# Attention and two expert layers in one kernel: raw weights staged in accumulators, values loaded ahead of keys, a smaller filler quota

## The chip, the cores and the metric

The kernel runs as one program on one core of a Trainium2 chip. The metric is device time in microseconds, the median of several runs. Engines are named as in the profile: PE (TensorE) with its weight loads PEld, DVE (VectorE), ACT (ScalarE), POOL (GpSimd) and SP (SyncE), which here only issues transfers.

## The reference

Everything is float32. Three layers follow one another over 2304 tokens of width 512:

```
attention: 4 batches, 8 heads of 64; 512 local and 32 global tokens per batch
  local queries see keys within 32 positions and the 32 global keys
  global queries see everything; softmax(q k^T / 8) v
experts 1: P = exp(x w_gate - max), eight times scaled by row sums and column sums
  out = sum over 8 experts e of P[:, e] * (relu(x w1[e]) w2[e])      w1 512x1024, w2 1024x512
layer 2: elu(x w_in) w_out                                            512x2048, 2048x512, 64-bit weights
```

## The kernel before

**Precision.** Each operand of a large product is split into a high and a low part (`split`, L121: ACT casts the high part, POOL subtracts to get the low part), and three products stand for one (`three`, L129: lines 131, 133 and 135 of the profile).

**Attention.** The 16 head pairs (4 batches by 4 pairs) run in a loop over p; a *pair* below is one turn of it, p = 0 to 16, and a *slot* is one of its eight steps i = 0 to 7. At the start of a turn PE gets the scores of pair p (`scores`, tile s) and the value products of pair p-1 (`pv`, tile o); in odd turns also the global queries' value products and scores (tiles o and sg). In slots 0, 1, 3 and 4 DVE takes the maxima and ACT the exponentials (`maxi`, tile e); in slots 4 and 6 PE transposes the exponentials (`transp`, tile ptp) and ACT copies them (tile pt). In slot 6 of odd turns `expo_g` runs the global exponentials on DVE and ACT (tile eg). In slot 7 of even turns outputs are transposed into the next layer's input x (`x_t`). Batches 0 and 1 of x stay in SBUF, the later ones are stored to scratch by `x_out` (tensors xdh and xdl).

**Filler.** Each slot ends with `fill_for(FILL)`: a generator (`filler`) that issues matmuls of the first expert layer as soon as a batch of x is there, until their planned durations reach the quota. It does unit 0 (half of expert 0) and then unit 1 for batches 0 and 1, in halves of 256 tokens: `mm1` (four groups of 12 matmuls into a bank of the pool psm, which has two; ACT's Relu writes hh, DVE writes hl), then `mm2_part` into a bank that is freed by the groups before, added into the accumulators `accs`. Before x exists (the first four turns), `busy` keeps PE at work with matmuls on zeros. What is left of the filler runs behind the attention. `logits` computes the gate for a batch (tiles lgp, lt, lgt), and when the last batch is through, the row and column sums of the gate (`sinkhorn`, matmul pcs on tile cs) are issued between other matmuls by a planned clock, one step about every 3.9 us; at the first completed output of unit 2 what is left of them is issued at once (`mix2`).

**Weights of units 0 and 1.** `load_unit` is a generator of ten steps: step i loads raw tile i (128x512, 256 KB) into a pool of three buffers and splits raw tile i-2 into wA. For unit 0 a step is taken in slots 1 and 5 of turns 0 to 4. For unit 1 the steps are taken inside `unit_plain`: two where the second half of unit 0 of batch 1 begins, four between its mm2 matmuls, four between the first mm1 matmuls of unit 1.

**Transfers.** All loads and stores are issued on SP in the order of the program: keys and queries of a pair (`load`, tile kq, 592 KB, three buffers), values (`load_vw`, tile vw, 910 KB, two buffers), values for the global queries (`load_vc`, tile vc, one buffer, odd turns), queries of the global tokens (qg). SP waits for a free buffer where none is there, and what is behind waits with it. Eight semaphores serve the transfers in turn. The masks, `first_sums` (tiles sfh and sfl) and the loads for unit 2 are on the same queue.

After the filler every further unit runs in `mix1` and `mix2`, with 512 columns per matmul, and then layer 2; nothing of that is touched.

Of the kernel before, what the change touches and what calls it, by code (L numbers as in the profile page):

```python
# [11 lines left out]
F32 = mybir.dt.float32  # L12
# [22 lines left out]
LEAST, MOST = (float(np.uint32(x).view(np.float32)) for x in (0x38000000, 0x47EFFFFF))  # L35
VN = HD + 1
LOC = B * SL
FILL = 750.0
LAG = 3900.0
AHEAD = (3, 5, 7, 9)  # L40
BACK = (15, 17, 19, 21)
# [19 lines left out]
def tile_net(ctx: ExitStack, tc, kq, vw, vc, qg, wg, w1, w2, wi, wo, consts, out):  # L61
    nc = tc.nc
# [41 lines left out]
    wA = {"1" + p: wall[p][:, :2048].rearrange("p (k f) -> p k f", k=4) for p in "hl"}  # L104
# [16 lines left out]
    def split(hi, lo, src, hi_eng="act", lo_eng="pool"):  # L121
        if hi_eng == "act":
            nc.scalar.copy(hi, src)  # L123
        else:
            nc.gpsimd.tensor_scalar(hi, src, 1.0, 1.0, op0=ALU.mult, op1=ALU.mult)
        e = nc.gpsimd if lo_eng == "pool" else nc.vector
        e.tensor_tensor(out=lo, in0=src, in1=hi.bitcast(F32), op=ALU.subtract)  # L127
# [39 lines left out]
    att = ExitStack()  # L167
# [13 lines left out]
    def load(p):  # L181
        a = kq_t[p] = apl.tile([128, NKS + SL], F32, tag="kq", name="kq")
        if p > 0:
            nc.sync.dma_start(a, kq[p])
            return
        for c in (slice(NKS, NKS + 128), slice(0, 192), None, slice(NKS + 128, None), slice(192, NKS)):
            if c is None:
                nc.sync.dma_start(masks, consts[:, 256:].rearrange("p (a f) -> p a f", a=4))
            else:
                nc.sync.dma_start(a[:, c], kq[0][:, c])  # L190
# [6 lines left out]
    def load_vw(p):  # L197
        v = ap2.tile([128, 2, NS - 2, VN], F32, tag="vw", name="vw")
        nc.sync.dma_start(v, vw[p])
        vw_t[p] = v  # L200

    def load_vc(g):
        c = ap1.tile([112, 4, 5, VN], F32, tag="vc", name="vc")
        nc.sync.dma_start(c, vc[g // 2, g % 2])
        vc_t[g] = c
# [27 lines left out]
    def transp(p, r):  # L233
        s = st[p, r]
        ptp = psr.tile([128, 512], F32, tag="r", name="ptp")
        for i in range(4):
            nc.tensor.transpose(ptp[:, i * 128:(i + 1) * 128], s["e"][:, i], ident)
        s["pt"] = ap3.tile([128, 512], F32, tag="pt", name="pt")
        nc.scalar.copy(s["pt"], ptp)

    def pv(p):
# [143 lines left out]
    def unit_plain(u, b, swap=None):  # L385

        for c0 in (0, 256):
            leave, come = (swap is not None and u == v and c0 == 256 * (1 - v) for v in (0, 1))
            hh, hl = (hs[p][:, :, c0:c0 + 256] for p in "hl")
            if leave:  # L390
                next(swap)
                next(swap)
            n = 0
            for r in mm1(wA, lambda p, k: xcols(p, k, b)[:, c0:c0 + 256], 256, hh, hl):
                yield r
                n += 1
                if come and n % 12 == 0:
                    next(swap, None)
            n = 0
            for o in (0, 128):  # L400
                i = b * 4 + (c0 + o) // 128
                ps = psm.tile([128, 512], F32, tag="m", name="m2")
                for r in mm2_part(wA, ps, hh, hl, o, range(4)):
                    yield r
                    n += 1
                    if leave and n % 6 == 0:
                        next(swap)
                if u == 0:
                    nc.vector.tensor_copy(accs[i], ps)
                else:  # L410
                    nc.vector.tensor_tensor(out=accs[i], in0=ps, in1=accs[i], op=ALU.add)
                yield "q"

    rawp = att.enter_context(tc.tile_pool(name="rawp", bufs=3, side="left"))

    def load_unit(u):

        raw = []
        for i in range(10):
            if i < 8:  # L420
                raw.append(rawp.tile([128, 512], F32, tag="raw", name="raw"))
                nc.sync.dma_start(raw[i], (w1, w2)[i // 4][u][:, i % 4])
            if i > 1:
                n, k = "12"[(i - 2) // 4], (i - 2) % 4
                split(wA[n + "h"][:, k], wA[n + "l"][:, k], raw[i - 2])
            yield

    def first_sums(k, c):
# [43 lines left out]
    with tc.manual_schedule():  # L472
        load(0)
        nc.sync.dma_start(ident, consts[:, 0:128])
        load_vw(0)
        load(1)
        load_qg(0)
        nc.sync.dma_start(ones, consts[:, 128:256])
        nc.sync.dma_start(wgf, wg)
        fill = filler()  # L480
        owed = [0.0]
        done = [False]

        def busy(n):

            for _ in range(n):
                nc.tensor.matmul(idle, zeros[:, :128], zeros, start=True, stop=True)

        lgen = {}

        def logits_part(b):

            if b not in lgen:
                lgen[b] = logits(b)
            for _ in takewhile(lambda r: r != "lag", lgen[b]):
                pass

        def fill_for(ns):
            owed[0] = min(owed[0] + ns, 2.0 * ns)
            while owed[0] > 0 and not done[0]:  # L500
                r = next(fill, "end")
                if r == "end":
                    done[0] = True
                elif r == "wait":
                    owed[0] = 0.0
                elif r == "lag":

                    owed[0] = -0.5 * ns
                elif r != "q":
                    owed[0] -= r  # L510

        zeros = hs["l"][:, 3, :512]
        nc.vector.memset(zeros.bitcast(F32), 0.0)
        idle = psm.tile([128, 512], F32, tag="m", name="idle")
        busy(START)
        unit0_weights = load_unit(0)
        ahead = deque(f for k in range(2) for c in range(4) for f in first_sums(k, c))
        for p in range(np_ + 1):
            live, odd, g = p < np_, p % 2 == 1, p // 2
            if live:  # L520
                scores(p)
            if p > 0:
                pv(p - 1)
                o0, o1 = (st[p - 1, r]["o"] for r in range(2))
            if odd:
                if g > 0:
                    global_pv(g - 1, o0[:, 384:384 + VN])
                scores_g(g, o0[:, 288:352])
                load_vc(g)
            if p + 2 < np_:  # L530
                load(p + 2)
            if p + 1 < np_:
                load_vw(p + 1)
            if p % 4 == 2 and p + 2 < np_:
                load_qg(p // 4 + 1)
            for i in range(8):
                if live and i in (0, 1, 3, 4):
                    if i == 4:
                        transp(p, 0)
                    for j in range(2):  # L540
                        maxi(p, i // 3, (i % 3) % 2 * 2 + j)
                if i == 2:
                    if p > 0:
                        norm(p - 1, 0)
                        norm(p - 1, 1)
                    if p == 0:
                        split(wgs[:, :, :E], wgs[:, :, E:], wgf)
                if i == 5 and odd and g > 0:
                    norm_g(g - 1)
                if i == 6:  # L550
                    if live:
                        transp(p, 1)
                    if odd:
                        expo_g()
                    elif p > 0:
                        copies = global_t(g - 1, o1[:, 384:512])
                if i == 7 and not odd and p > 0:
                    copies()
                    x_t(g - 1)
                    if g % 2 == 0:  # L560
                        b = g // 2 - 1
                        st["xready", b] = True
                        if b > 1:
                            x_out(b)
                if i in (1, 5) and p < 5:
                    next(unit0_weights, None)
                if p < H // 2:
                    busy(WARM)
                fill_for(FILL)
                if st.get(("xready", 1)):  # L570
                    pop(ahead)
                if p == 13 and i in (0, 4):
                    logits_part(2)
        og = psr.tile([128, 512], F32, tag="r", name="og")
        global_pv(B * 2 - 1, og[:, :VN])
        norm_g(B * 2 - 1)
        pop(ahead, len(ahead))
        x_tg()
        x_out(B)
        for b in (B - 1, B):  # L580
            for _ in range(2):
                logits_part(b)
                for _ in range(14):
                    next(fill, None)
# [765 lines left out]
```

## Time and profile before

| | us |
|---|---|
| median of 3 runs | 1956.5 (1956.34 to 1960.3) |
| profiled execution | 1957.93 |
| its span, first to last instruction | 1956.2 |
| PE busy | 1901.3 (97%) |
| DVE busy | 1430.7 (73%) |
| ACT busy | 768.8 (39%) |
| POOL busy | 670.5 (34%) |
| raw tiles, issue to landing | 2.8 to 10.4, median 7.2 |

PE is busy nearly all the time over the whole span, but not evenly: the page's row of forty slices begins with 7897989 and goes on with nines. The clock that PE was granted is below full in the first slice and in single short stretches. A busy share of PE therefore says less than the idle time in front of single PE instructions, with the name of what ended it, and the clock of the stretch behind.

### The profile page before, as it was taken

What the parts mean: (1) busy time and instruction counts of PE and PEld (TensorE: products, weight loads), DVE (VectorE), ACT (ScalarE), POOL (GpSimd) and SP (SyncE); (2) the same over time, 40 slices, a digit from 0 to 9 for tenths busy, and PEclk for the clock granted to TensorE, in tenths of its full rate; (3) what the DMA queues carried; (4) which work ended last, traced back from release to release, by engine and by line L of the source; (5) the groups of instructions that cost most, each with busy time, mean ns of one, the idle gap of its engine ahead of it and who ended that gap; (6) DMA issues with size and microseconds to landing.
All of it is one profiled execution on the core that took longest, in us unless ns stands there. A gap on an engine that the chain in (4) does not pass through costs nothing. (4 is left out here: it accounts for less than half of the span.)

```text
span 1956.2 us, 32431 instructions
## 1 busy us (share of the span) xinstructions
PE 1901.3 (97%) x12315; PEld 1638.1 (84%) x12315; DVE 1430.7 (73%) x2707; ACT 768.8 (39%) x1599; POOL 670.5 (34%) x581
## 2 busy tenths in 40 slices
PE   7897989999999999999999999999999999999999
PEld 5776768888888888899999999999999977789998
DVE  3454476676776767687878787888888677778887
ACT  4444333333322323233333333333333244545654
POOL 1035222333223333344435353555455112223322
PEclk9899999999999999999999999999999999999999
DMA  6556521332223322623343434333333495554432
GB/s 238 177 176 216 196 76 44 97 104 77 100 80 108 103 76 76 234 87 111 116 122 113 123 109 133 98 108 99 101 103 103 126 293 166 168 213 139 121 118 71
DMA packets 200716, 250.30 MB, mean 128 GB/s; under 512 B 16752, under 2 KB 150128, under 8 KB 200560
## 3 DMA queue, kind: packets, MB, share of 16 engines
q1 hardware_dynamic: 200560, 248.23, 39.6%
q8 instruction: 97, 1.59, 0.3%
q14 instruction: 59, 0.48, 0.1%
HBM read 189.32 MB, written 58.85 MB: 127 GB/s over the span
## 5 line engine op out<-in xcount | busy, mean ns | idle before, releaser
L131 PE MATMUL m<-w2h,hh 128*128 128x512 f32 x1360 | 534.6, 393 | 6.9 <-DVE hl L140 4.7
L135 PE MATMUL m<-w2h,hl 128*128 128x512 f32 x1360 | 535.0, 393 | 2.5 <-POOL hl L1003 2.5
L133 PE MATMUL m<-w2l,hh 128*128 128x512 f32 x1360 | 534.2, 393 | 0.0
L972 ACT ACTIVATE hh<-t 128x288 fp32r<-128x288 f32 (+1 forms) x368 | 184.9, 502 | 437.0 <-DVE t L966 432.6
L135 PEld LDWEIGHTS m<-w2h,hl 128*128 128x128 f32 x1360 | 256.6, 189 | 59.6 <-POOL hl L1003 5.8
L131 PEld LDWEIGHTS m<-w2h,hh 128*128 128x128 f32 x1360 | 257.1, 189 | 57.5 <-DVE hl L140 5.3
L133 PEld LDWEIGHTS m<-w2l,hh 128*128 128x128 f32 x1360 | 257.0, 189 | 50.8
L974 DVE SCALAR_TENSOR_TENSOR hl<-t,hh 128x288 fp32r<-128x288 f32 (+1 forms) x368 | 283.2, 770 | 4.0 <-ACT hh L972 0.2
L1074 DVE SCALAR_TENSOR_TENSOR acc<-m,pr,acc 128x512 f32<-128x512 f32 x247 | 183.2, 746 | 116.2 <-PE m L135 116.2
L127 POOL TENSOR_TENSOR w2l<-w2r,w2h 128x512 fp32r<-128x512 f32 x120 | 162.7, 1380 | 299.9 <-ACT w2h L123 284.9
L966 DVE TENSOR_TENSOR t<-q,u 128x288 f32<-128x288 f32 (+1 forms) x348 | 182.9, 526 | 62.2 <-PE q L1033 52.9
L1003 POOL TENSOR_TENSOR hl<-eg,hh 128x288 fp32r<-128x288 f32 (+2 forms) x112 | 103.7, 934 | 290.2 <-ACT hh L1002 189.8
L690 ACT CAST wh<-wt 128x512 fp32r<-128x512 f32 x120 | 68.9, 619 | 239.0 <-POOL wt L686 239.0
L686 POOL TENSOR_TENSOR wt<-w1r,wt 128x512 f32<-128x512 f32 x60 | 89.5, 1492 | 203.0 <-DVE hl L974 107.5
L686 POOL TENSOR_TENSOR wt<-w1r 128x512 f32<-128x512 f32 x60 | 79.9, 1335 | 174.7 <-DVE hl L974 124.6
L1014 DVE TENSOR_TENSOR u<-q,s 128x288 f32<-128x288 f32 (+1 forms) x116 | 61.2, 528 | 86.0 <-PE q L1033 61.7
L694 DVE TENSOR_TENSOR wl<-wt,wh 128x512 fp32r<-128x512 f32 x120 | 106.9, 901 | 14.6 <-ACT wh L690 12.9
L1222 DVE TENSOR_TENSOR acc<-m,acc 128x512 f32<-128x512 f32 x105 | 72.1, 688 | 32.8 <-PE m L135 32.5
L760 POOL TENSOR_TENSOR cp<-r,cp 128x512 f32<-128x512 f32 x32 | 42.7, 1335 | 144.0 <-DVE cp L750 73.3
L1012 ACT COPY s<-q 128x288 f32<-128x288 f32 (+1 forms) x116 | 52.0, 448 | 77.6 <-PE q L1033 77.6
L694 DVE TENSOR_TENSOR wl<-w1r,wh 128x512 fp32r<-128x512 f32 x90 | 81.3, 903 | 0.0
L984 ACT ACTIVATE er<-t 128x288 f32<-128x288 f32 (+1 forms) x96 | 48.5, 505 | 81.3 <-DVE t L966 81.2
(238 smaller groups left out, 4160.8 us busy)
## 6 DMA issues: line engine op xcount, KB each, us to landing
w1r<-in_w_dram SPq DMA_DIRECT2D x60, 512.0 KB, 4.9
w2r<-in_w_dram SPq DMA_DIRECT2D x60, 512.0 KB, 3.7
vw<-in_vw_dram SPq DMA_DIRECT2D x16, 910.0 KB, 6.7
wh<-wqh SPq DMA_DIRECT2D x98, 128.0 KB, 2.7
wl<-wql SPq DMA_DIRECT2D x98, 128.0 KB, 2.7
kq<-in_kq_dram SPq DMA_DIRECT2D x15, 592.0 KB, 7.1
r<-in_wo_dram SPq DMA_DIRECT2D x16, 512.0 KB, 3.9
r<-in_wi_dram SPq DMA_DIRECT2D x16, 512.0 KB, 3.6
```

The source lines that it names most:

```text
L127: e.tensor_tensor(out=lo, in0=src, in1=hi.bitcast(F32), op=ALU.subtract)
L131: nc.tensor.matmul(ps, ah, bh, start=first, stop=False)
L133: nc.tensor.matmul(ps, ah, bl, start=False, stop=False)
L135: nc.tensor.matmul(ps, al, bh, start=False, stop=last)
L686: eng.tensor_tensor(out=t, in0=get(a), in1=get(b), op=op)
L694: eng.tensor_tensor(out=wop[n + "l"], in0=src, in1=wop[n + "h"].bitcast(F32), op=ALU.subtract)
L966: nc.vector.tensor_tensor(out=t, in0=ps, in1=rest, op=ALU.add)
L972: nc.scalar.activation(hh, t, AF.Relu)
L974: late.append(lambda: nc.vector.scalar_tensor_tensor(out=hl, in0=t, scalar=0.0, in1=hh.bitcast(F32), op0=ALU.max, op1=ALU.subtract))
L1003: nc.gpsimd.tensor_tensor(out=hl, in0=g[:, a:b], in1=hh.bitcast(F32), op=ALU.subtract)
L1074: nc.vector.scalar_tensor_tensor(out=accs[i], in0=ps, scalar=scale, in1=accs[i], op0=ALU.mult, op1=ALU.add)
L1222: nc.vector.tensor_tensor(out=acc, in0=ps, in1=acc, op=ALU.add)
```

## The change

The quota of a slot falls from 750 to 650. Raw tiles of unit 0 are loaded into the accumulators accs[0] to accs[7], which are not used until the first output of the filler; for unit 1 the pool gets five buffers instead of three, five tiles are loaded in slots 0 to 4 of turn 6, and the last three when the first three splits free a buffer. `load_unit` now has eight steps, each a split. The first split of unit 0 stands in turn 1, slot 1, as before. The pt tile moves to a pool of two buffers. Keys of pair 1 are loaded ahead of the values of pair 0 at the start; in the loop the order becomes values, keys, global values. The split of the gate's weights (wgs) moves from turn 0 to turn 2.

```diff
-FILL = 750.0
+FILL = 650.0
...
-        s["pt"] = ap3.tile([128, 512], F32, tag="pt", name="pt")
+        s["pt"] = ap2.tile([128, 512], F32, tag="pt", name="pt")
...
-            if leave:
-                next(swap)
-                next(swap)
...
-    rawp = att.enter_context(tc.tile_pool(name="rawp", bufs=3, side="left"))
+    rawp = att.enter_context(tc.tile_pool(name="rawp", bufs=5, side="left"))
+    raw = {}
+
+    def load_raw(u, i):
+        raw[u, i] = accs[i] if u == 0 else rawp.tile([128, 512], F32, tag="raw", name="raw")
+        nc.sync.dma_start(raw[u, i], (w1, w2)[i // 4][u][:, i % 4])
 
     def load_unit(u):
 
-        raw = []
-        for i in range(10):
-            if i < 8:
-                raw.append(rawp.tile([128, 512], F32, tag="raw", name="raw"))
-                nc.sync.dma_start(raw[i], (w1, w2)[i // 4][u][:, i % 4])
-            if i > 1:
-                n, k = "12"[(i - 2) // 4], (i - 2) % 4
-                split(wA[n + "h"][:, k], wA[n + "l"][:, k], raw[i - 2])
+        for i in range(8):
+            n, k = "12"[i // 4], i % 4
+            split(wA[n + "h"][:, k], wA[n + "l"][:, k], raw[u, i])
+            if u == 1 and i < 3:
+                load_raw(1, i + 5)
             yield
...
+        load(1)
         load_vw(0)
-        load(1)
...
-                load_vc(g)
+            if p + 1 < np_:
+                load_vw(p + 1)
             if p + 2 < np_:
                 load(p + 2)
-            if p + 1 < np_:
-                load_vw(p + 1)
+            if odd:
+                load_vc(g)
...
-                    if p == 0:
+                    if p == 2:
                         split(wgs[:, :, :E], wgs[:, :, E:], wgf)
...
-                if i in (1, 5) and p < 5:
+                if i in (1, 5) and p < 4:
+                    load_raw(0, 2 * p + i // 4)
+                if i in (1, 5) and 0 < p < 5:
                     next(unit0_weights, None)
+                if p == 6 and i < 5:
+                    load_raw(1, i)
```

Three places in the order of the instructions. The first is SP's queue around the stores of x (xdh, xdl), in turns 12 to 14; raw is a raw tile of unit 1, sfh and sfl are partial sums. Before:

```order
L422 DMA raw<-in_w_dram 128x512 x3
L354 DMA xdh<-hh 512x1x512
L354 DMA xdl<-hl 512x1x512
L204 DMA vc<-in_vc_dram 112x1300
L184 DMA kq<-in_kq_dram 128x1184
L199 DMA vw<-in_vw_dram 128x1820
L422 DMA raw<-in_w_dram 128x512
L446 DMA sfh<-hh 512x1x128
L446 DMA sfl<-hl 512x1x128
L422 DMA raw<-in_w_dram 128x512
```

And after the change:

```order
L354 DMA xdh<-hh 512x1x512
L354 DMA xdl<-hl 512x1x512
L199 DMA vw<-in_vw_dram 128x1820
L184 DMA kq<-in_kq_dram 128x1184
L204 DMA vc<-in_vc_dram 112x1300
L416 DMA raw<-in_w_dram 128x512
L445 DMA sfh<-hh 512x1x128
L445 DMA sfl<-hl 512x1x128
L416 DMA raw<-in_w_dram 128x512 x2
```

Two raw tiles stood behind the stores before, the seventh and eighth of unit 1; three do now, the sixth to the eighth, and values go ahead of keys and global values.

The second is ACT's queue in turn 7, from the exponentials of the second head on (e); m is a bank of the filler, hh the Relu of a group, eg the global exponentials. Before:

```order
L231 ACTIVATE e<-e,m 128x128 x2
L139 ACTIVATE hh<-m_1432 128x256
L239 COPY pt<-ptp 128x512
L295 ACTIVATE eg<-sg,mg 128x480
L295 ACTIVATE eg<-o,mg 128x64
L139 ACTIVATE hh<-m_1462 128x256
L139 ACTIVATE hh<-m_1498 128x256
L231 ACTIVATE e<-e,m 128x128 x6
```

And after the change:

```order
L231 ACTIVATE e<-e,m 128x128 x2
L139 ACTIVATE hh<-m_1420 128x256
L239 COPY pt<-ptp 128x512
L295 ACTIVATE eg<-sg,mg 128x480
L295 ACTIVATE eg<-o,mg 128x64
L139 ACTIVATE hh<-m_1449 128x256
L231 ACTIVATE e<-e,m 128x128 x4
L139 ACTIVATE hh<-m_1485 128x256
L231 ACTIVATE e<-e,m 128x128 x2
L139 ACTIVATE hh<-m_1584 128x256
```

Before, the last two groups of a half stood directly behind the global exponentials; now one group does, and the last two stand in the next turn, between its exponentials.

The third is PE's queue at the end of the column sums, in the first mix2 of unit 2; q is a product of mix1, m an output bank, pcs the column sums. Before:

```order
L135 MATMUL m_3875<-w2h,hl 128x512
L1031 MATMUL q_3816<-xs4h,wh 128x512
L1032 MATMUL q_3816<-xs4l,wh 128x512
L1033 MATMUL q_3816<-xs4h,wl 128x512
L1031 MATMUL q_3816<-xs4h,wh 128x512
L1032 MATMUL q_3816<-xs4l,wh 128x512
L1033 MATMUL q_3816<-xs4h,wl 128x512
L924 MATMUL pcs<-cs,ones 128x8 x2
L131 MATMUL m_3850<-w2h,hh 128x512
```

And after the change:

```order
L1037 MATMUL q_3852<-x22h,wl 128x512
L131 MATMUL m_3864<-w2h,hh 128x512
L133 MATMUL m_3864<-w2l,hh 128x512
L135 MATMUL m_3864<-w2h,hl 128x512
L131 MATMUL m_3864<-w2h,hh 128x512
L133 MATMUL m_3864<-w2l,hh 128x512
L135 MATMUL m_3864<-w2h,hl 128x512
L928 MATMUL pcs<-cs,ones 128x8
L131 MATMUL m_3876<-w2h,hh 128x512
```

The last two column sums stood together behind the product q before; now the last one stands alone, between matmuls of mix2, and the one before it 18 matmuls earlier.

## Rows read from the trace of the kernel before

**Rows 1.** Busy time by stage: stretch, length, PE, PEld, DVE, ACT, POOL busy, clock, DMA.

```profile
0.00:62.60 62.60, 43.91 (x775) 30.95 (x775) 21.38 (x123) 28.50 (x70) 11.52 (x15) 0.86 0.64 222
62.60:218.50 155.90, 139.21 (x2566) 118.47 (x2565) 76.71 (x361) 73.94 (x186) 47.78 (x78) 0.98 0.53 175
244.00:285.00 41.00, 32.89 (x138) 25.66 (x137) 32.54 (x87) 12.32 (x21) 9.70 (x7) 0.92 0.24 83
285.00:1956.20 1671.20, 1662.79 (x8716) 1445.30 (x8714) 1289.56 (x2109) 647.61 (x1308) 597.64 (x478) 1.00 0.38 119
```

**Rows 2.** PE's waits, 62.6 to 285: waiting for what, total us, times, longest.

```profile
PE pcs L924 <- DVE cs L919: 8.1, 6, 2.5
PE lgt L377 <- DVE hl L140: 6.5, 2, 6.2
PE m L131 <- DVE hl L140: 5.5, 5, 2.2
...
PE ptp L237 <- ACT e L231: 0.6, 1, 0.6
```

**Rows 3.** PE's waits, 0 to 62.6.

```profile
PE o L251 <- issue: 8.3, 2, 4.2
PE ptp L237 <- ACT e L231: 5.5, 9, 2.4
```

**Rows 4.** Timeline, turn 13 to 14: start, length, engine, line, what, [idle before <- releaser].

```profile
160.84 1.16 PE L216 MATMUL s<-kq 64*32 64x128 f32 x64
...
162.56 0.53 SPq L354 DMA_DIRECT2D xdh<-hh  x1
...
168.25 0.93 SPq L422 DMA_DIRECT2D raw<-in_w_dram  x1
...
178.62 0.62 ACT L123 CAST w2h<-raw 128x512 fp32r<-128x512 f32 x1 [5.58 <-DMA raw<-in_w_dram]
...
180.04 0.61 PE L377 MATMUL lgt<-ident,lt 16*128 16x16 f32 x4 [6.22 <-DVE hl L140]
...
185.71 1.16 PE L216 MATMUL s<-kq 64*32 64x128 f32 x64
```

**Rows 5.** Busy time and clock of three short stretches.

```profile
178.49:185.32 6.83, 5.28 (x19) 4.58 (x20) 3.10 (x12) 4.88 (x11) 4.46 (x7) 0.50 0.07 22
277.47:284.30 6.83, 4.34 (x12) 3.48 (x12) 3.74 (x14) 3.46 (x6) 0.00 (x0) 0.50 0.00 0
...
40.00:60.00 20.00, 13.58 (x291) 10.07 (x290) 8.93 (x55) 10.76 (x27) 5.44 (x5) 0.80 0.61 212
```

**Rows 6.** Timeline, turn 0: the gate's weights and the transposes behind.

```profile
12.30 0.22 ACT L123 CAST wgs<-wgf 128x32 fp32r<-128x32 f32 x1 [2.70 <-DMA wgf<-in_wg_dram]
...
12.88 0.62 PE L237 MATMUL ptp<-ident,e 128*128 128x128 f32 x2 [2.42 <-ACT e L231]
```

**Rows 7.** Timeline, end of turn 7: ACT and PE.

```profile
99.19 0.66 ACT L295 ACTIVATE eg<-sg,mg 128x480 f32<-128x480 f32 x1 [2.02 <-DVE mg L293]
...
99.95 0.66 ACT L139 ACTIVATE hh<-m 128x256 fp32r<-128x256 f32 x2
...
100.84 0.49 PE L131 MATMUL m<-w2h,hh 128*128 128x512 f32 x1 [2.20 <-DVE hl L140]
```

**Rows 8.** Timeline, PE: first and last two of six column sums that waited.

```profile
255.74 0.39 PE L924 MATMUL pcs<-cs,ones 128*128 128x8 f32 x2 [1.31 <-DVE cs L919]
...
277.17 0.39 PE L924 MATMUL pcs<-cs,ones 128*128 128x8 f32 x2 [2.15 <-DVE cs L919]
280.05 0.59 PE L924 MATMUL pcs<-cs,ones 128*128 128x8 f32 x2 [2.49 <-DVE cs L919]
```

**Rows 9.** Timeline, PE, turn 6: the two groups of transposes.

```profile
79.25 0.60 PE L237 MATMUL ptp<-ident,e 128*128 128x128 f32 x4
...
81.31 1.05 PE L237 MATMUL ptp<-ident,e 128*128 128x128 f32 x4
```

**Rows 10.** Timeline, PE: the second wait without a releaser.

```profile
54.01 0.88 PE L251 MATMUL o<-vw,pt 128*32 128x65 f32 x23 [4.22 <-issue]
```

**Rows 11.** DMA queues, 49 to 55 us: packets, MB, share of 16 engines.

```profile
q8 instruction: 1, 0.02, 0.9%
```

## Prediction

> **What bounds the kernel now.** I read the busy times by stage first [rows 1]. From 285 us to the end PE is busy 1662.79 of 1671.2 us: nothing in the change reaches there, so that stage only shifts. What can move is the first 285 us: 43.91 of 62.6 us busy with a clock of 0.86 while no filler exists, 139.21 of 155.9 with filler, 32.89 of 41.0 around the column sums of the gate. PE is the engine that is filled, so each idle microsecond of PE in front of 285, and each stretch in which its clock is halved, is time of the kernel. The second view is the list of PE's waits in these stages [rows 2 and 3]: 8.1 us for the column sums (pcs), 6.5 for lgt of which one wait is 6.2, 5.5 for m, and in front of that 8.3 us in which PE waited for nothing that the profile shows, and 5.5 us for exponentials. Third, the timeline around the longest ones, to see who was really late.
>
> The 6.2 us wait at 180.04 is put down to DVE, but ACT shows the cause [rows 4]: it stood 5.58 us in front of CAST w2h until a raw tile landed, at 178.6. That tile was asked for at 168.25, behind the stores of x, which began at 162.56. ACT works in order, so the Relu that frees the filler's bank, and with it DVE and PE, stood behind that cast. Right behind the wait the clock is 0.50 for 6.83 us [rows 5].
>
> The sum is made against the profiled execution, 1957.9 us (1956.2 span and 1.7 around it), which is 1.4 above the median of 1956.5.
>
> **The change part by part.**
>
> *Gate split.* In pair 0 ACT waited 2.70 us for the gate's weights, and PE 2.42 us for the exponentials behind them [rows 6]. In pair 2 these weights are long there; the cast (0.22 us) then stands between exponentials of a stage that waits anyway. What is late next are keys and values of pair 1; the keys now go ahead, and the cast of raw tile 0 may have to wait for its tile, but PE's global scores lie over that. -2.2; bounds -2.7 and 0.
>
> *Raw tiles of unit 0 in the accumulators, five buffers for unit 1.* The eight casts of unit 0 stay in the same slots (both generators reach the first split in pair 1, slot 1); only the third-buffer wait of SP goes. For unit 1 five tiles come in pair 6, and three come after the splits that free a buffer. The order shows where: tile 5 is still issued behind the stores, vw, kq and vc, and its cast stands in pair 14, behind that pair's first four exponentials. Before, the late tile landed 178.6 - 160.84 = 17.8 us after the start of pair 13 [rows 4]; the same bytes stand in front of tile 5, so I take 17.8 again. Pair 13 lasted 185.71 - 160.84 = 24.9 us; without the wait (6.2), the half clock behind it (half of 6.83, 3.4) and eight slots that are 0.1 shorter, 14.5. The cast stands some 3 to 4 us into pair 14 (the pair's score and value products, then 17 filler matmuls), so at 17.5 to 18.5: the tile is just there. Tiles 6 and 7 are wanted 3 us later still. I keep 0.5 us of the wait: -(6.2 + 3.4 - 0.5) = -9.1; bounds -9.6, and -4 if ACT still stands some 5 us.
>
> *Less filler per slot: where a half unit ends.* In pair 7 and pair 11 the fourth mm1 group ended in slot 6 or 7 of an odd pair, where ACT has the global exponentials first: hh of the last two groups came behind them at 99.95, and PE waited 2.2 us for a bank (100.84) [rows 7]. With 0.4 before each, this makes 5.2 of the 5.5 us of m's row [rows 2]. In the new order the halves end in pairs 6, 8, 10, 12 and 14, which have no global exponentials; behind those of pair 7 ACT has only one Relu. -4.5, since other places can pinch; bounds -5.2 and 0.
>
> *Less filler per slot: what moves.* From slot 7 of pair 4 to slot 7 of pair 16 there are 97 slots, 9.7 us of filler by the planner's count, and the order has 165 filler matmuls behind the transposes of xg where it had 106. On PE that is the same work in another place, 0. It matters at two ends. Behind the gate's logits there is more filler for the column sums to hide in: before, the four that stood alone and waited cost 8.1 - 2.15 - 2.49 = 3.5, 0.9 each, and the last two were issued as a pair because the schedule ran out, 2.15 and 2.49 [rows 2 and 8]. Now all eight stand alone, three of them in the filler. I leave four at 0.9: 8.1 falls to 3.5, -4.6, and take half of the 3.4 us that the half clock from 277.47 on cost [rows 5]: -6.3 in all; bounds -11.5 (all of both) and 0.
>
> The other end is the cover of the exponentials. In pair 6 the second four transposes took 1.05 us where the first took 0.60 [rows 9], so PE stands there already. Six slots before them are shorter by 0.1 each: up to 0.6 us in each of 11 pairs, 6.6; I take +3.5, bounds 0 and +6.6.
>
> *Values ahead of keys, global values last.* Each of these tiles is used a pair or two later (kq and vw in the next pair but one, vc likewise), and PE's only wait for them was the first keys, so the direct price is 0. pt with two buffers costs nothing: the value products that free one stand in front of the transposes that fill it. What does change is when transfers run. PE's two longest waits of the first stage, 4.2 us each, have no releaser, and in the one before 54.01 the core's DMA engines moved an instruction packet [rows 3, 10, 11] while keys loaded early for an even pair were under way. These keys now come later. -1; bounds -8 (both waits gone) and +4 (one more like them).
>
> The Trainium skill, Runtime: NRT & Kernel Launch, section Instruction fetch mechanics, holds that crossing an instruction block costs one DMA that is mostly hidden. By it this term would be 0 and the sum 1 us higher; the trace has 4.22 us there that nothing else explains.
>
> *Sum.* -2.2 - 9.1 - 4.5 - 6.3 + 3.5 - 1.0 = -19.6; 1957.9 - 19.6 = 1938.3, and I say 1938.
>
> **The rivals.**
>
> *The raw tile is late again.* For it: tile 5 still stands behind two stores of 1 MB, and its cast now has exponentials of the same pair right behind it. Against it: its place is a pair later. If its wait and the half clock stay whole but for 0.5 us: 1938.3 + 8.6 = 1947.
>
> [...]
>
> *The chain binds, not PE.* With less filler each pair lasts as long as DVE, ACT and the transposes need; the cover costs its full 6.6, and the column sums, which are a DVE chain, wait as before. For it: the 0.45 us in pair 6 and DVE busy in 32.54 of the 41 us in question [rows 1 and 9]. Against it: only 0.6 us of waits for exponentials in 156 us [rows 2]. 1938.3 + 3.1 + 6.3 = 1948.
>
> *The instruction waits go too.* With nothing early under way in the even pairs, both 4.2 us waits vanish: 1938.3 - 7 = 1931.
>
> *Nothing is won.* The filler's places are dealt anew, and waits of the same size appear elsewhere; the moved matmuls are neutral: 1956 to 1959.
>
> *Slower: the clock falls in the attention stage.* One mechanism: PE's gaps between the shorter slots grow until the clock is halved again and again. It has a price in the trace: with no filler the clock was 0.80 from 40 to 60 us, with filler it is 0.98 over 155.9 us [rows 1 and 5]. At 0.80, 0.18 of the roughly 147 us that are left of this stage, 26 us: 1938.3 + 26 = 1964. It decides from a mean clock of about 0.84 on, where it eats the whole gain (0.14 x 147 = 21). Against it: a slot still holds 0.65 us of filler, and the stage's waits for exponentials are short.
>
> **How the numbers follow.** The forecast has 0.57, the late tile 0.15, the chain 0.12, the instruction waits 0.06, nothing won 0.05, the clock 0.05. The forecast's own range is 1932 to 1944 (the bounds of six terms, not all at one end). For 8 in 10 I go from 1928, below the instruction waits' case, to 1951, above the late tile and the chain, and leave out the last two cases and some of the edges. A change of 0.2%, 3.9 us, is about what can be told from none; faster than that are the first four cases but for some mixture of their worst ends: 0.88. Within 0.2% 0.07, slower 0.05.
>
> **What would show it.** ACT has no wait over 1 us for a raw tile after 100 us, and PE no idle of 6 us in front of lgt; if ACT stands at a cast of w2h in pair 14, the tile was late. PE's waits for m from DVE fall from 5.5 to under 2. The column sums wait under 5 in all, without a pair of over 2 us at the end, and the clock record of 6.83 us at their end is gone or not. The transposes' waits in the filler stage rise from 0.6 to a few us; far more says that the chain binds. The mean clock from pair 5 to the end of the attention stays at 0.96 or above; under 0.84 the slower case is on. From the first mix2 on both traces run alike, so the difference must be there before some 285 us; if it arises later, the forecast is wrong even with the right size.

## The result and the profile after

The changed kernel takes 1934.07 us (median of 4 runs, 1931.73 to 1934.49), the kernel before 1956.42 (4 runs, 1955.12 to 1960.3): a ratio of 0.988, 95% interval 0.9863 to 0.9897. Forecast were 1938 and a range of 1928 to 1951. The profiled executions differ by 23.4 us (1934.49 against 1957.93, spans 1932.7 and 1956.2), the sum of the forecast was 19.6. The table goes by stretch, between instructions that both kernels have, and is worked out from the two traces. In the brackets, *idle* is the sum of PE's gaps and *half* is how long the clock stood at the lower of its two levels (0.50 in the records, 1.2 GHz), both in us:

| stretch | before: us (idle, half) | after: us (idle, half) | difference | forecast |
|---|---|---|---|---|
| start to scores of turn 5 | 62.62 (18.7, 17.1) | 58.22 (15.7, 10.2) | -4.40 | -3.2 |
| to the first transposes of xg | 155.86 (16.7, 6.8) | 140.89 (11.4, 3.4) | -14.97 | -10.1 with the next |
| to the first product q | 27.35 (3.0, 3.4) | 33.86 (1.3, 0) | +6.51 | |
| to the first q of unit 3 | 54.24 (8.1, 6.8) | 44.81 (1.5, 0) | -9.43 | -6.3 |
| rest | 1656.09 (8.4, 6.8) | 1654.94 (8.4, 4.1) | -1.15 | 0 |

The second and third stretch belong together, since the filler that leaves the slots stands in the third: -8.46. So one stretch gave 1.6 us less than forecast, and the others 1.2, 3.1 and 1.15 more. The rest differs by the clock: its gaps are the same, and the record at half clock in its course is 6.83 us long in the trace of before (at 1608.7) and 3.41 in the other (at 1587.3).

Busy time by stage of the changed kernel, columns as in [rows 1], and last one short stretch:

```profile
0.00:58.20 58.20, 42.53 (x775) 29.90 (x775) 21.27 (x123) 28.60 (x70) 11.49 (x15) 0.91 0.72 239
58.20:199.10 140.90, 129.49 (x2506) 108.24 (x2505) 73.98 (x357) 72.06 (x183) 47.47 (x78) 0.99 0.60 194
232.90:277.80 44.90, 43.42 (x193) 34.64 (x192) 35.41 (x76) 18.01 (x31) 13.15 (x9) 1.00 0.23 78
277.80:1932.70 1654.90, 1646.57 (x8649) 1431.81 (x8647) 1281.84 (x2096) 641.56 (x1298) 593.70 (x476) 1.00 0.38 119
153.66:157.07 3.41, 3.41 (x20) 1.79 (x18) 1.85 (x10) 0.00 (x0) 0.00 (x0) 0.50 1.02 335
```

Around the column sums PE is busy 43.42 of 44.9 us at full clock. The clock of the attention stage is 0.99, far from the 0.84 at which the slower rival would have decided. PE's waits of the changed kernel, 58.2 to 277.8, against [rows 2]:

```profile
PE sg L284 <- issue: 3.8, 2, 2.5
PE m L135 <- POOL wl L127: 2.3, 2, 1.2
PE m L131 <- DVE hl L140: 1.8, 2, 1.1
...
PE pcs L928 <- DVE cs L923: 1.2, 1, 1.2
...
PE ptp L237 <- ACT e L231: 0.8, 2, 0.6
PE lgt L377 <- DVE hl L140: 0.2, 1, 0.2
```

The column sums fell from 8.1 to 1.2, lgt behind DVE from 6.5 to 0.2, m behind DVE from 5.5 to 1.8. New is a wait for POOL, which makes the low parts of the weight splits (wl). The waits marked `issue` are those without a releaser. Timeline of the changed kernel at the end of turn 13, where the tile was late before [rows 4]:

```profile
160.87 0.60 ACT L123 CAST wh<-raw 128x512 fp32r<-128x512 f32 x1
...
164.71 1.27 POOL L127 TENSOR_TENSOR wl<-raw,wh 128x512 fp32r<-128x512 f32 x1
...
166.03 0.38 PE L135 MATMUL m<-x11h,wl 128*128 128x256 f32 x1 [1.24 <-POOL wl L127]
...
170.41 0.39 PE L135 MATMUL m<-x12h,wl 128*128 128x256 f32 x1 [1.07 <-POOL wl L127]
```

ACT waits for no raw tile here; PE waits for the subtraction that POOL ran from 164.71 to 165.98, of a high part that had been cast at 160.87. POOL has other sums in front of it and no gap from 160.45 to 176.70. The first stage, PE's waits from 0 to 62.6, against [rows 3]:

```profile
PE o L251 <- issue: 6.4, 2, 3.7
PE sg L284 <- issue: 3.3, 1, 3.3
PE ptp L237 <- ACT e L231: 3.1, 8, 0.5
```

Turns 0 and 1 of the changed kernel on PE, against [rows 6], and then the global scores of turn 1 in the kernel before:

```profile
11.85 0.62 PE L237 MATMUL ptp<-ident,e 128*128 128x128 f32 x2 [0.29 <-ACT e L231]
...
18.71 0.81 PE L284 MATMUL sg<-kq,qg 128*32 128x192 f32 x11 [3.34 <-issue]
```

```profile
20.25 0.81 PE L284 MATMUL sg<-kq,qg 128*32 128x192 f32 x11 [1.31 <-issue]
```

The 2.42 us wait for exponentials is gone, but the wait without a releaser in front of the global scores grew from 1.31 to 3.34. PE arrived there 3.6 us earlier than before (15.37 against 18.94) and left only 1.5 us earlier.

The last sum of the changed kernel, the only one that waits, against [rows 8]:

```profile
255.59 0.39 PE L928 MATMUL pcs<-cs,ones 128*128 128x8 f32 x2 [1.25 <-DVE cs L923]
```

### The profile page after: what moved, and what is told of

Same layout as the page of the kernel before. It is cut to its first block, busy times and chain, and to the rows that moved or that the text cites. A ratio compares the mean times of both kernels' runs of the same rounds, so it can differ in the third digit from the quotient of the medians.

```text
span 1932.7 us, 32414 instructions
## 1 busy us (share of the span) xinstructions
PE 1894.5 (98%) x12315; PEld 1631.9 (84%) x12315; DVE 1431.6 (74%) x2707; ACT 767.8 (40%) x1599; POOL 669.7 (35%) x581
## 5 line engine op out<-in xcount | busy, mean ns | idle before, releaser
L698 DVE TENSOR_TENSOR wl<-wt,wh 128x512 fp32r<-128x512 f32 x120 | 106.9, 901 | 14.5 <-ACT wh L694 12.8
```

The source lines that it names most:

```text
L698: eng.tensor_tensor(out=wop[n + "l"], in0=src, in1=wop[n + "h"].bitcast(F32), op=ALU.subtract)
```

## The experiments

Theory: the quota's gain comes from the filler that is left behind the logits and from where the half units end; the staged tiles' gain from the late tile; the gate split's from turn 0. Rivals are stated with each run. The four runs of the first group shared a chip and its runs of the kernel before (1957.35), the next four another (1957.5), the last four a third (1955.87). Each ratio is to the kernel before on the same chip.

**The change with the old quota.** `-FILL = 650.0`, `+FILL = 750.0`.

> The changed kernel with the quota back at 750; loads, order and gate split as changed. Theory (three independent gains: staged raw tiles 9, smaller quota some 12 at the column sums and some 5 at the half units, start 3 to 4): without the quota's share 1946, with column sums waiting about 8 us again, a half clock behind them, and two waits of PE for m of about 2 us in turns 7 and 11, but no wait of ACT for a raw tile over 1 us. Rival (the quota is worth nothing, the loads do it all): 1934.

1945.25 us (1944.24 to 1947.83), ratio 0.9942 (0.9927 to 0.9957). PE's waits, 56 to 290:

```profile
PE pcs L928 <- DVE cs L923: 8.1, 6, 2.5
PE m L131 <- DVE hl L140: 5.1, 4, 2.2
```

Both waits of before are back; the second line has 2.20 and 2.21 us in turns 7 and 11. Without the quota the change is worth 12.1 us; the quota adds about 11 to it. ACT has no wait for a raw tile after 100 us.

**The quota alone, in the kernel before.** `-FILL = 750.0`, `+FILL = 650.0`.

> The kernel before with the quota at 650 and nothing else. Theory: column sums wait under 2 us as in the changed kernel, the waits for m in turns 7 and 11 go, but the raw tiles of unit 1 are now asked for behind the stores in their majority, so ACT still waits 5 us or more for one of them in turn 13 or 14 and PE with it: 1943 to 1948. Rival (the quota does it all): 1934 to 1937. Second rival (without the staged tiles the smaller quota gains nothing, since later raw loads cost what the column sums win): 1955 or more.

1937.92 us (1934.99 to 1939.53), ratio 0.9901 (0.9886 to 0.9916): a miss for the theory by 5 us and more. One number gives 19.4 of the 22.3 us, though a raw tile is late again (another one than before). Timeline of this kernel around turn 14:

```profile
166.98 1.26 POOL L127 TENSOR_TENSOR wl<-raw,wh 128x512 fp32r<-128x512 f32 x1
168.20 0.62 ACT L123 CAST wh<-raw 128x512 fp32r<-128x512 f32 x1 [3.40 <-DMA raw<-in_w_dram]
168.20 1.00 POOL L441 TENSOR_TENSOR acc<-acc 128x128 f32<-128x128 f32 x2
168.30 0.39 PE L135 MATMUL m<-x11h,wl 128*128 128x256 f32 x1 [1.23 <-POOL wl L127]
169.16 1.29 POOL L127 TENSOR_TENSOR wl<-raw,wh 128x512 fp32r<-128x512 f32 x1
...
172.68 0.39 PE L135 MATMUL m<-x12h,wl 128*128 128x256 f32 x1 [1.08 <-POOL wl L127]
...
180.55 0.62 ACT L123 CAST w2h<-raw 128x512 fp32r<-128x512 f32 x1 [1.92 <-DMA raw<-in_w_dram]
```

ACT stands 3.40 us for a tile, and PE does not notice: it waits 1.23 and 1.08 us for POOL, exactly where it does in the changed kernel (1.24 and 1.07), in which ACT does not stand at all. POOL works without a gap of 0.1 us from 162.70 to about 179; its queue covers the late tile. Only the second tile, 1.92 us late and behind the end of that stretch, costs PE something: 0.66 us, at 181.96. At the old quota POOL had gaps here, 1.5 to 4.9 us each, and ACT's 5.58 us reached PE as 6.2 us. From the trace of before:

```profile
179.32 1.27 POOL L127 TENSOR_TENSOR w2l<-raw,w2h 128x512 fp32r<-128x512 f32 x1 [4.92 <-ACT w2h L123]
```

**The gate split back in turn 0.** In the changed kernel `-if p == 2:`, `+if p == 0:` at the split of the gate's weights.

> The changed kernel with the gate split back in turn 0. Theory: PE waits 2.4 us for the exponentials of turn 0 again, and the wait without a releaser in front of the global scores of turn 1 falls from 3.34 to about 1.3, since it ends at a fixed time; so of 2.4 us only 0.5 to 1.5 reach the end: 1935. Rival (the whole of it reaches the end): 1936.5.

1936.02 us (1934.85 to 1936.78), ratio 0.9893 (0.9878 to 0.9907), 1.9 above the change; theory and rival are too close for the time to tell them apart. The timeline of PE does:

```profile
13.16 0.77 PE L237 MATMUL ptp<-ident,e 128*128 128x128 f32 x2 [3.00 <-ACT e L231]
...
15.77 1.96 PE L216 MATMUL s<-kq 64*32 64x128 f32 x64
...
19.40 1.22 PE L284 MATMUL sg<-kq,qg 128*32 128x192 f32 x16
```

The wait for exponentials is back with 3.00 us, and the one in front of the global scores is gone: PE comes there at 19.40, later than the 18.71 at which it was let go in the changed kernel. So that wait does not end at a fixed time, as the theory had it (20.25 before, 21.62 with the quota alone). PE's idle time up to the scores of turn 5 is the same with the split in turn 0 as without, 15.94 and 15.67 us: what the move saves in front of the transposes is paid in front of the global scores. The stage is still 3.1 us longer (61.33 against 58.22), and the difference lies in the clock: 20.48 us at half clock against 10.24. One of these records begins with the end of the 3.00 us wait (13.03 to 19.86), and the scores of turn 1 take 1.96 us in it, 1.16 in the changed kernel. That rests on two profiles, and the time at half clock in this stage is not steady: a second profile of the changed kernel has 17.07 us of it, in a stage of 59.09.

**The tiles and buffers alone.** The changed kernel with quota 750, the old load order and the gate split in turn 0.

> The kernel before with the raw tiles staged (accumulators, five buffers, five loads in turn 6, pt in two buffers); quota 750, old order of the loads, gate split in turn 0. Theory: the 5.58 us of ACT and 6.2 us of PE in turn 13 go, with the half clock behind: 1957.9 - 9.1 = 1949. Rival (another late tile takes its place, the stores are still in front of three tiles): 1955 to 1958.

1950.96 us (1948.31 to 1953.4), ratio 0.9967 (0.9954 to 0.998): -6.4, near the theory. Busy time of turn 13, of the kernel before and then of this one, columns as in [rows 1]:

```profile
160.84:185.71 24.87, 16.77 (x260) 13.58 (x259) 8.26 (x38) 11.32 (x27) 12.71 (x18) 0.86 0.67 224
```

```profile
166.50:182.20 15.70, 14.38 (x260) 11.59 (x259) 7.93 (x38) 8.13 (x21) 9.92 (x14) 1.00 0.92 311
```

The same 260 matmuls take 9.2 us less, the -9.1 of the forecast; but turns 8, 10 and 12 are 1.5, 1.2 and 1.5 longer, records at half clock begin at 103.8 and 155.0 where there was none, and the stage from turn 5 to xg gains 4.8 only. Waits for the sums and for m stay:

```profile
PE pcs L928 <- DVE cs L923: 8.2, 6, 2.5
PE m L131 <- DVE hl L140: 5.5, 5, 2.2
```

From the first run, the change with the quota of 750, this one differs by the gate split and the load order alone. The two are worth 5.7 us there (1950.96 against 1945.25), most of it in the first stage (63.89 against 57.46 us in the profiles).

**The change with the old load order.** In each turn the global values, then keys and queries of the turn after next, then values, as before; at the start the values of pair 0 ahead of the keys of pair 1.

```diff
+        load_vw(0)
         load(1)
-        load_vw(0)
...
+            if odd:
+                load_vc(g)
+            if p + 2 < np_:
+                load(p + 2)
             if p + 1 < np_:
                 load_vw(p + 1)
-            if p + 2 < np_:
-                load(p + 2)
-            if odd:
-                load_vc(g)
```

> The changed kernel with the old order of the loads (keys and queries ahead of values, global values first, values of pair 0 ahead of keys of pair 1). Theory: the order only shifts when transfers run in the first stage; PE waits for none of these tiles, so 1932 to 1937, with p5 (the scores of turn 5) between 57 and 62 us. Rival (the order is what shortens the waits without a releaser, as in the prediction's term of -1, or as the 5.7 us between the loads-only kernel and the quota-750 kernel would have it): 1938 to 1940, with the two long waits back at 4.1 and 4.2 us.

1931.72 us (1929.3 to 1934.7), ratio 0.987 (0.9855 to 0.9884). The order earns nothing; the rival of 1938 to 1940 is wrong.

**Six warm-up matmuls fewer.** `-START, WARM = 9, 1`, `+START, WARM = 3, 1`, one run, to see what PE's waits without a releaser hang on.

> The changed kernel with 3 in place of 9 warm-up matmuls at the start (work on zeros; the result does not depend on it). In all traces so far PE's waits without a releaser stand in front of its 220th, 346th, 601st and 727th matmul. Theory (they are PE waiting for its next block of instructions): they stand in front of the same numbers again, so six matmuls later in the program: in front of the 10th of the 24 sg matmuls in turn 1, behind 31 in place of 25 value products in turn 2, and behind 47 in place of 41 in turn 4. Rival (they are waits for a tile that the profile does not name): they stay in front of the 4th sg matmul and behind 25 and 41 value products. Time 1932 to 1938.

1933.34 us. PE's timeline around the waits, first in the changed kernel (its first wait, 3.34 us at 18.71, is shown above), and then in this one:

```profile
25.32 0.58 PE L251 MATMUL o<-vw,pt 128*32 128x65 f32 x25
28.65 0.77 PE L251 MATMUL o<-vw,pt 128*32 128x65 f32 x39 [2.74 <-issue]
45.09 0.81 PE L251 MATMUL o<-vw,pt 128*32 128x65 f32 x41
```

```profile
15.04 0.73 PE L284 MATMUL sg<-kq,qg 128*32 128x192 f32 x9
17.95 0.45 PE L284 MATMUL sg<-kq,qg 128*32 128x288 f32 x4 [2.19 <-issue]
24.37 0.65 PE L251 MATMUL o<-vw,pt 128*32 128x65 f32 x31
28.19 0.67 PE L251 MATMUL o<-vw,pt 128*32 128x65 f32 x33 [3.17 <-issue]
44.08 0.88 PE L251 MATMUL o<-vw,pt 128*32 128x65 f32 x47
49.13 0.45 PE L251 MATMUL o<-vw,pt 128*32 128x65 f32 x17 [4.16 <-issue]
```

All three waits moved by six matmuls, from behind 3, 25 and 41 products to behind 9, 31 and 47. They stand behind PE's first 220, 346 and 727 matmuls in both kernels, and in the kernel before: where they stand goes by the place in the instruction stream, not by what is loaded.

**A still smaller quota.** `-FILL = 650.0`, `+FILL = 550.0`.

> The changed kernel with a quota of 550. Theory: the column sums lie in filler altogether and wait for less than 1.5 us, a gain of 1 at most; the attention turns come near their chain of exponentials, so waits for e rise by 3 us or more: 1934 to 1939. Rival (still bound by the placing of filler, the smaller the better): 1925 to 1931.

1939.76 us (1937.89 to 1941.24), ratio 0.9907 (0.989 to 0.9923), just above the theory's range. No column sum waits, but in the attention stage there are 10.3 us at half clock, and PE waits for the chain:

```profile
PE ptp L237 <- ACT e L231: 5.0, 7, 1.0
PE lgt L377 <- DVE hl L140: 2.2, 1, 2.2
```

**The smaller quota in the last turns alone.** 750 up to turn 12, 450 from turn 13: `fill_for(750.0 if p < 13 else 450.0)`.

> The changed kernel with a quota of 750 up to turn 12 and 450 from turn 13 on, so that as much filler as in the changed kernel is left behind the attention, but turns 5 to 12 are as at 750. Theory (12 of the quota's gain come from what is left behind the gate's logits): column sums wait under 2 us and no half clock follows; the two waits of 2.2 us for m in turns 7 and 11 stay, so 1945.3 - 12 + 0 to 4 = 1933 to 1937. Rival (the gain comes from the placing in turns 5 to 12): 1942 or more.

1939.21 us (1938.61 to 1940.96), ratio 0.9909 (0.9894 to 0.9923), between theory and rival: of the some 11 us of the quota about 6 come with the last turns (1945.25 to 1939.21), on another chip, and not 12. PE's waits:

```profile
PE m L131 <- DVE hl L140: 4.4, 2, 2.2
...
PE pcs L928 <- DVE cs L923: 1.7, 2, 1.4
```

The column sums need only filler behind the logits, wherever it was saved: the stretch from the first q to unit 3 is 45.17 here, 44.81 in the changed kernel, 53.87 with 750. The half units need the smaller quota in the early turns: both 2.2 us waits for m stay.

**The change again,** unedited, and **the old load order again,** beside two other quotas with the old order.

> The changed kernel once more, beside the next three on the same chip: 1931 to 1936. Its difference to the next one says whether the new order of the loads is worth anything; theory: nothing, within 3 us of the next.

> The changed kernel with the old order of the loads, once more: 1929 to 1935. Theory (the order is worth nothing): within 3 us of the changed kernel in this call. Rival (the new order costs): at least 3 us faster than it again.

1935.09 us (1930.52 to 1935.5), ratio 0.9889 (0.9874 to 0.9904), and 1931.89 (1930.73 to 1932.28), ratio 0.9877 (0.9861 to 0.9894). The intervals overlap, but the old order is lower twice, by 2.4 us on another chip and by 3.2 on the same, and its stage from turn 5 to xg is shorter in both profiles: 136.93 and 136.77 against 140.89 and 141.18. There is a half clock of 3.41 us in that stage in both profiles of the change and none in either of the old order. The new order as a whole seems to cost some 3 us. Where, the profiles show; PE's waits without a releaser from 56 to 290, in the change run again and then in the old order run again:

```profile
PE sg L284 <- issue: 4.9, 2, 2.7
...
PE o L251 <- issue: 0.6, 1, 0.6
```

```profile
PE sg L284 <- issue: 3.0, 2, 2.5
```

They stand behind 1364, 2380 and 2635 matmuls, that behind 2380 in the new order alone (at this quota), and come to 5.0 and 5.5 us in the two profiles of the change, 3.1 and 3.0 in those of the old order. That is PE's whole difference in idle time in the stage (1.9 and 2.4 us). The half clocks, which begin right behind two of these waits, make the rest of it: PE is busy 2.1 and 2.0 us longer with the same matmuls. Why the waits are longer in the new order is open.

**The old order with quotas of 690 and of 600.**

> Old order of the loads with a quota of 690. By the order, six of the eight column sums stand in products and mix2, none as a pair, and no half unit ends in an odd turn. Theory (what counts is that filler is left behind the logits and that no half ends in front of the global exponentials): column sums wait 2 to 4 us, no wait of 2.2 us for m, 1931 to 1937. Rival (each 40 of quota cost in proportion, 12 us per 100): 1936 to 1940.

> Old order of the loads with a quota of 600. Theory: column sums wait about 0 to 1 us, waits for exponentials (ptp) and half clocks rise half way to those at 550: 1932 to 1938. Rival (650 is still too much): 1926 to 1930.

1936.22 us (1933.94 to 1937.26), ratio 0.9899 (0.9884 to 0.9913), and 1937.04 (1935.88 to 1941.57), ratio 0.9909 (0.9894 to 0.9924). PE's longest wait, first with 690, then with 600:

```profile
PE m L135 <- POOL wl L127: 4.0, 2, 3.6
```

```profile
PE m L135 <- POOL wl L127: 3.4, 2, 1.8
```

The time with 690 fits theory and rival alike; that with 600 is in the theory's range, but the transposes wait 1.1 us for exponentials, little more than at 650. In both POOL's low parts are late, which no expectation had, and the attention stage has 10.2 and 6.8 us at half clock; the sums wait little (1.5 and 0.8 us). With the old order 650 is better than 600 and 690, with the new one better than 550 and 750. The change with the old load order is the fastest version run.

## Why the prediction was right, and where it was not

The side and the size were right, 1934.07 for 1938, and so was the place: the difference is there when unit 3 begins, but for 1.15 us. The terms were not all right, and that the sum came so close is in part luck. The forecast has 7.3 us for the quota and 12.3 for all the rest. Run alone they gave 19.4 and 12.1, and together 22.3: the quota's terms were 12.1 too small, an overlap of 9.2 between the two was left out, and most of the one error cancels the other.

*Column sums: too small.* The steps that failed are "I leave four at 0.9" and the half of one half clock. One wait of 1.25 is left of 8.1, and both half clocks, at 222.86 and at 277.47, are gone: -9.43 in their own stretch where -6.3 stood, and in the stretch before it the idle falls from 3.0 to 1.3 and 3.4 us at half clock disappear. The mistake was to leave the chain its 0.9 us wherever a sum stands alone. The chain is not equally long everywhere: from the end of one sum to the cs of the next it takes 2.4 to 2.5 us where the sums stand in the filler, and 4.2 to 5.5 where DVE has work of the products and of mix2 in between. In the changed kernel three of the seven steps are of the short kind and stand in PE's order with more than their 2.4 us of other work between them; before, one was, besides the last pair, whose whole chain PE waited for. In the changed kernel two sums are 4.4 to 5.9 us apart, and seven of the eight wait less than 0.1 us. Tried both ways: 8.1 and 8.2 us stay with the old quota, 1.2 and 1.7 when only the quota, or only its last turns, change.

*Raw tiles: right alone, wrong in the sum.* Turn 13 loses 9.2 us when the tiles are staged at the old quota, and -9.1 was forecast. But the kernel gained only 6.4, and at the new quota little: the stage from turn 5 to xg takes 138.49 us with the quota alone, and 136.93 and 136.77 with staged tiles in the same order of loads. The quota alone already takes the wait from PE, since POOL's queue is then the last to finish. The terms for the tiles and for the quota were added as if independent; that is the main error of the working. The forecast had the tile just there. It landed 16.7 us after the start of turn 13, for 17.8, and its cast came 7.2 us later, at 171.64, mostly since turn 13 took 18.6 us and not 14.5; ACT has no wait for a raw tile after 100 us.

*Half units: right, with a successor.* Both 2.2 us waits are gone, and turns 7 and 11 are 4.1 and 4.3 us shorter. They return with the quota of 750 and where only the last turns have less. "Other places can pinch" was right, and the place was not named: 2.3 us for POOL's wl, and 1.08 for hl behind it.

*Cover of the exponentials: too dear.* +3.5 were set down; PE waits 0.8 us for exponentials in the attention stage, where it was 0.6. At 550 it is 5.0. So 650 stands above the edge that the rival "the chain binds" described.

*Gate split: about right, by another way.* -2.2 forecast; the run with the split put back is 1.9 and 0.9 above the two medians of the change, on other chips. In the profiles the first stage takes 61.33 to 64.29 us in all four with the split in turn 0 and 56.20 to 59.54 in all ten with it in turn 2. The 2.4 us of idle time came back as a wait in front of the global scores; what the run with the split put back loses there is lost at half clock.

*Order of the loads: wrong sign.* -1 was taken for waits without a releaser, with transfers as the cause. The waits stay (9.7 us in the first stage, 9.6 before), and the sixth run ties their places to the instruction's number. The order is worth nothing there, and costs some 3 us behind it, through longer waits of the same kind in the attention stage; the bound of +4 had that. The Trainium skill, Runtime: NRT & Kernel Launch, section Instruction fetch mechanics, holds that PE's instructions come in blocks and that crossing one is mostly hidden. The waits at fixed numbers fit blocks, but no run shows that these are their cause; if they are, the traces contradict that they are hidden, with 2.74, 3.34 and 3.67 us.

Open stays why waits at the same places in the instruction stream are longer with one order of loads than with another.

## What to carry to other kernels

Two repairs of one wait are not worth their sum: before adding terms, ask what is late when the first is done, and whether the second still reaches the engine that counts; here POOL's full queue hid a tile that came 3.4 us late. Work that can be placed freely is best kept for the stretch in which the busy engine would wait for a chain, and the place where it pinches is found by trying the share in steps, since 750 loses 11 us and 550 loses 6. A wait without a releaser is tested by shifting the instruction count: what moves with the number keeps its place under another order of loads, though its length can change (5.0 and 5.5 us in the attention stage against 3.1 and 3.0).

## What the runs showed of the hardware

PE stands behind its first 220, 346 and 727 matmuls for 1.3 to 4.5 us with no releaser in the trace, in every profile of this case, whatever the order of the loads, but for the one with the split put back, which has no wait behind 220. What the length goes by is not shown: behind 220 it was 3.34 us where PE came at about 15.4, 1.31 where it came at 18.94 and none where it came at about 19.4, but 3.19 with the quota alone, where it came at 18.43. Work saved in front of such a place can be lost again there. And the clock is unsteady at the margin: behind the same wait of 2.2 us for m there is no record at 0.50 in the kernel before, and two of 3.41 us each (at 103.8 and 155.0) in the kernel with the staged tiles alone.
